# A two-branch attention kernel: the query combine of one branch redone, score banks freed in pairs, and a new instruction order

## Chip, cores, metric

One core of a Trainium2 chip. The metric is the device time of one launch in microseconds. "Before" and "changed" name the two kernels throughout. A launch is called slow when it is over 1.5% above the fastest of its kernel; every profiled launch was fast. Medians and ranges below are over all launches. Same, faster and slower are at 2%.

## The reference, cut to what matters

Both branches read the same x (2048 tokens, 640 columns, 32 heads of 20); a sigmoid gate g mixes them. Branch A is linear attention with a feature map made of two softmaxes:

```python
pq = einsum('bhsd,hdf->bhsf', q, w_phi)                 # pk the same from k
phi_q = concatenate([softmax(pq), softmax(-pq)], -1)    # 40 features per head
kv  = einsum('bhsf,bhsd->bhfd', phi_k, v);  z = phi_k.sum(s)
num = einsum('bhqf,bhfd->bhqd', phi_q, kv)
den = einsum('bhqf,bhf->bhq', phi_q, z) + 1e-6
a = (num / den) @ wo
# branch B: causal softmax attention in 4 segments of 512 tokens, plus a memory term, @ wo
return g * a + (1 - g) * b
```

Write E+ for exp(pq), E- for exp(-pq), Z+ and Z- for their sums over a head's 20 features. Since num and den are both linear in phi_q, a common factor cancels: multiply by Z+, and only E- needs the ratio r = Z+/Z-. Both kernels use that. They differ in where the ratio is applied.

In all views PE is TensorE's matmuls and PEld its weight loads, DVE is VectorE, ACT ScalarE and POOL GpSimd. SBUF is the on-chip memory; PSUM is the memory that TensorE writes to, here eight banks, handed out singly, as four pairs, or four banks at once. Evacuating means copying a result out of PSUM.

## The kernel before

The program is a list of operations with priorities and estimated durations. A scheduler in the kernel's own Python lays them out greedily on each engine when the program is built, and gives them SBUF slots and PSUM banks. A "step" is one group of four heads in one segment of branch B: 32 steps, each with three bursts of score matmuls, five exponentials, four masks and an attention product. Everything else (projections, branch A) fills in between as "fillers". "Burst N" below, and in the prediction, is the first score burst of step N.

```python
def d_act(n): return 0.22 + n * 0.000833            # the scheduler's estimates, us
def d_mm(*ns): return sum(max(n / 2400.0 + 0.004, 0.034) for n in ns)
...
MAXPAIRS = 2                                        # bank pairs that fillers may hold
def filler_ok(self, fillers, t):
    ...
    return len(pairs) <= self.MAXPAIRS              # one-bank tiles
    return len(pairs) < self.MAXPAIRS               # two-bank tiles
...
def burst(js):                                      # in b_step: scores of four heads
    pt = self.pst("QK", 5 if js[0][0] == 2 else 4)  # ONE tile of four banks
    ...
def expair(pt, off, j):
    for p in range(2):                              # two exponentials, two banks each
        self.op("act", d_act(1024), ..., W=[(pt, 2*p), (pt, 2*p+1), (ex, (j, p))])
...
# in a_q(S): query work of branch A, per tile of 128 tokens and half hf of the heads
pt = self.pst("U", 2)                               # bank 0: E+ part, bank 1: E- part
# 22 columns a head: 20 of num, den, and the plain sum Z
recip   sm0 = 1 / U-[:, :, 21]                      # VectorE, 16 elements
mult    sm1 = U+[:, :, 21] * sm0                    # r
mult    W   = U-[:, :, 0:21] * r                    # 336 elements from PSUM
add     W   = W + U+[:, :, 0:21]                    # 336 elements from PSUM
recip   sm2 = 1 / W[:, :, 20]
stt     oA  = W[:, :, 0:20] * g * sm2               # 320 elements
```

The last six lines are VectorE instructions written as formulas; the whole kernel has them as code.

The softmax here doesn't subtract the row's maximum and nothing guards it: scores larger than these inputs give would overflow.

Of the kernel before, what the change touches and what calls it, by code (L numbers as in the profile page):

```python
# [13 lines left out]
D = 640  # L14
# [16 lines left out]
def d_act(n):  # L31
    return 0.22 + n * 0.000833
# [6 lines left out]
def d_pool(n, ins=1):  # L39
    return 0.22 + n * 0.00087 * ins  # L40


def d_mm(*ns):
    return sum(max(n / 2400.0 + 0.004, 0.034) for n in ns)
# [7 lines left out]
class Tile:  # L52
    def __init__(self, name, shape, dtype, pool):
        self.name, self.shape, self.dtype, self.pool = name, shape, dtype, pool
        self.ops = []
        self.h = {}
        self.slot = None
        self.prev = ()
        self.t = None
        self.left = 0  # L60
# [39 lines left out]
class Graph:  # L100
# [33 lines left out]
    def schedule(self):  # L134
# [21 lines left out]
        def dep_time(o, e):  # L156
            m = 0.0
            for d in o.deps:
                t = d.end
                if d.stream == e and e == "pe" and not d.dma:  # L160
                    continue
                if d.dma:
                    t = d.end + 0.1
                elif d.stream != e:
                    t += LAT
                else:
                    t += 0.03
                if t > m:
                    m = t
            return m  # L170

        def tile_avail(t, commit=False):
# [5 lines left out]
            if isinstance(p, PsumPool):  # L178
# [18 lines left out]
                if n == 2:  # L197
                    if not pairs or not self.filler_ok(fillers, t):
                        return None
# [34 lines left out]
        def claim_banks(t, bs):  # L234
# [6 lines left out]
            if t.shape < 4:  # L241
                fillers.add(t)

        def est(o, e):
            st = max(free[e], dep_time(o, e))
            for t in o.claim:
# [4 lines left out]
            for t in o.tiles:  # L251
# [5 lines left out]
                elif t.prev:  # L257
                    for d in t.prev:
                        if d.stream != e:
                            st = max(st, d.end + LAT)  # L260
# [74 lines left out]
    MAXPAIRS = 2  # L335
# [110 lines left out]
class GatedMix(Graph):  # L446
# [40 lines left out]

    def memory(self):
# [19 lines left out]
        self.KVZ1 = fx("KVZ1", [128, 2, NCH, 8, 22], BF16)  # L508
# [14 lines left out]
        self.onec = fx("onec", [128, 1], BF16)  # L523
        self.p_exp = self.pool(2, 10240)
# [11 lines left out]
        self.p_W = self.pool(2, 1344)  # L536
# [4 lines left out]
        self.p_as = self.pool(4, 192)  # L541
# [40 lines left out]
    def dma(self, q, o, i, R=(), W=(), pr=0.0, nbytes=0, transpose=False, noncontig=False, name="dma", after=(), claim=()):  # L582
# [8 lines left out]
        return self.op(q, 0.6 if q != "pool" else 1.0, fn, R, W, pr, name=name, dma=True, lat=2.0 + nbytes / 180e3, after=after, claim=claim)  # L591

    def setup(self):
# [5 lines left out]
        for s in range(SEG):  # L599
            sl = slice(LSEG * s, LSEG * (s + 1))  # L600
            self.dma("sp", xT[:, :, sl], x2d[sl, :], W=[(xT, s)], pr=-30 + 2.5 * s, nbytes=655e3, transpose=True, name=f"x{s}")
            if s == 0:
                self.dma("sp", self.wkT[:, :, :], wqkv[0:D, D:2 * D], W=[(self.wkT, "*")], pr=-29, nbytes=819e3, transpose=True, name="wkT")
        self.dma("sp", self.wqT[:, :, :], wqkv[0:D, 0:D], W=[(self.wqT, "*")], pr=-15, nbytes=819e3, transpose=True, name="wqT")
        self.dma("act", self.stq[:, :, :], wsrc(ins["B_wq"]), W=[(self.stq, "*")], pr=-40, nbytes=819e3, name="stq")
        self.dma("act", self.stk[:, :, :], wsrc(ins["B_wk"]), W=[(self.stk, "*")], pr=-39, nbytes=1638e3, name="stk")
        self.dma("act", self.WvB[:, :, 0:D], wsrc(ins["B_wv"]), W=[(self.WvB, "w")], pr=-38, nbytes=2400e3, name="WvB")
        self.dma("pool", self.WvB[:, :, D:D + 1], ins["gate_w"].rearrange("(c p o) -> p c o", p=128, o=1), W=[(self.WvB, "g")], pr=-40, noncontig=True, name="gw")
        self.dma("pool", self.beta[:, :], ins["B_beta"].partition_broadcast(128), W=[(self.beta, "*")], pr=-39, noncontig=True, name="beta")
        self.dma("pool", self.wphi[:, :, :], ins["A_w_phi"].rearrange("h d f -> (h d) f").rearrange("(c p) f -> p c f", p=128), W=[(self.wphi, "*")], pr=-38, noncontig=True, name="wphi")  # L610
        self.dma("act", self.WvA[:, :, :], wsrc(wqkv[:, 2 * D:3 * D]), W=[(self.WvA, "*")], pr=-30, nbytes=2400e3, name="WvA")
# [30 lines left out]
        op("act", 0.3, lambda e: e.activation(gh2[:, 1, :], self.beta[:, :], ACT.Exp, scale=-1.0), R=[(self.beta, "*")], W=[(gh2, "*")], pr=-20)  # L642
        op("dve", 0.1, lambda e: e.tensor_scalar(gh2[:, 1, :], gh2[:, 1, :], 1.0, None, op0=ALU.add), W=[(gh2, "*")], pr=-20)
        op("dve", 0.4, lambda e: e.reciprocal(gh2[:, 1, :], gh2[:, 1, :]), W=[(gh2, "*")], pr=-20)
        op("dve", 0.1, lambda e: e.tensor_scalar(gh2[:, 0, :], gh2[:, 1, :], -1.0, 1.0, op0=ALU.mult, op1=ALU.add), W=[(gh2, "*")], pr=-20)
# [5 lines left out]
        op("dve", 0.2, lambda e: e.tensor_copy(self.KVZ1[:, 0, :, :, 21], Mk[:, :, :]), R=[(Mk, "*")], W=[(self.KVZ1, "o0")], pr=2)  # L651
        op("dve", 0.2, lambda e: e.tensor_copy(self.KVZ1[:, 1, :, :, 21], Mk[:, :, :]), R=[(Mk, "*")], W=[(self.KVZ1, "o1")], pr=2)
# [7 lines left out]
    def fuse(self, wT, Wd, ic, pr):  # L660
# [12 lines left out]
        self.op("pe", 6 * 0.075, mm, R=[(wT, "*"), (BD, "*")], W=[(pt, 0), (pt, 1)], pr=pr, name="fuse")  # L673
# [3 lines left out]
    def evac(self, n, o, i, W, pr, name="ev", R=()):  # L677
        op = self.op(("act", "dve"), {"act": d_act(n), "dve": d_dve(n, 1, True)}, None, R=R, W=W, pr=pr, name=name)
# [67 lines left out]
    def b_mem(self, n):  # L746
# [7 lines left out]
        for tl in range(4):  # L754
# [9 lines left out]
            self.op("pe", 8 * 0.065, tr, R=rk + [(self.ident, "*")], W=[(pt, 0)], claim=[pk, tm], pr=pr, name="ktr")  # L764
            self.op("act", d_act(1024), lambda e, pt=pt, pk=pk: e.activation(pk[:, :], self.pb(pt, 0, 0, 1024), ACT.Exp),
                    W=[(pt, 0), (pk, "*")], pr=pr, name="pkexp")
            self.op("dve", d_dve(1024, 1, True), lambda e, pt=pt, tm=tm: e.tensor_scalar(tm[:, :], self.pb(pt, 0, 0, 1024), 1.0, 1.0, op0=ALU.add, op1=ALU.max),
# [14 lines left out]
        self.op("pe", 32 * 0.05, mm, R=[(p, "*") for p in pks] + [(vt, tl) for tl in range(4)] + [(vt, "one")], W=[(mp, 0), (mp, 1)], pr=pr, name="Mmm")  # L782
# [32 lines left out]
    def b_step(self, n, g):  # L815
# [7 lines left out]
        def burst(js):  # L823
            pt = self.pst("QK", 5 if js[0][0] == 2 else 4)

            def mm(e):
                for (j, c0) in js:
                    N = LSEG - 128 * j
                    for i in range(4):
                        r = e.matmul(self.pf(pt, i, c0, N), lhsT=qk[32 * i:32 * i + DH, g, 1, 128 * j:128 * (j + 1)],  # L830
# [3 lines left out]
            self.op("pe", 0.18 + sum((LSEG - 128 * j) / 2400.0 + 0.05 for j, _ in js), mm, R=rqk, W=[(pt, i) for i in range(4)], claim=[ex], pr=s, name=f"QK{n},{g}")  # L834
            return pt

        def expair(pt, off, j):
            for p in range(2):
                self.op("act", d_act(1024), lambda e, p=p: e.activation(  # L839
                    ex[:, 2 * p:2 * p + 2, off:off + 512], self.pbanks(pt, 2 * p, 2, 512), ACT.Exp, scale=scale),  # L840
                    W=[(pt, 2 * p), (pt, 2 * p + 1), (ex, (j, p))], pr=s + 0.01 * p, name="exp")
# [11 lines left out]
        p2 = burst([(2, 0)])  # L853
# [10 lines left out]
        for b in range(2):  # L864
# [25 lines left out]
            self.op("pe", cnt * 0.034 + (0.1 if am else 0), pv, R=R, W=[(ad, b)], pr=s + 0.9, claim=[self.oB], name=f"PV{n},{g}")  # L890
# [47 lines left out]
    def b_out(self, n):  # L938
        oB = self.oB
        for qi in range(4):  # L940
# [4 lines left out]
            def tr(e, qi=qi, pt=pt):  # L945
                for c in range(NCH):
                    r = e.transpose(self.pb(pt, 0, 128 * c, 128), oB[:, qi, 128 * c:128 * (c + 1)], self.ident[:, :])
                return r
            self.op("pe", 5 * 0.065, tr, R=[(oB, (g, qi // 2)) for g in range(NG)] + [(self.ident, "*")], W=[(pt, 0)], claim=[oT], pr=pr, name="oTBtr")
            self.evac(640, lambda oT=oT: oT[:, :, :], lambda pt=pt: self.pb(pt, 0, 0, 640).rearrange("p (c s) -> p c s", s=128),  # L950
                      W=[(pt, 0), (oT, "*")], pr=pr, name="oTB_ev")
            self.oTB[4 * n + qi] = oT

    def a_k(self, t):
        pr = 0.8 + 0.75 * t
# [33 lines left out]
    def a_kv(self, S):  # L989
        pr = 0.8 + 0.75 * (4 * S + 4)  # L990
        ts = [4 * S + i for i in range(4)]
        for s in range(2):
# [9 lines left out]
            self.op("pe", 20 * 0.075, mm, R=[(self.Et[t], s) for t in ts] + [(self.vt[t], "*") for t in ts], W=[(pt, 0), (pt, 1)], pr=pr, name="kv")  # L1002
# [11 lines left out]
        def half(hf, first):  # L1014
            lo = 64 * hf
            for k, t in enumerate(ts):
# [4 lines left out]
                else:  # L1021
                    self.op("dve", d_dve(1280, 2), lambda e, src=src: e.tensor_tensor(acc[lo:lo + 64, :], acc[lo:lo + 64, :], src(), ALU.add),  # L1022
# [6 lines left out]
    def a_fin(self):  # L1029
        pr = 12.9  # L1030
# [20 lines left out]
    def load_wo(self):  # L1051
        wsrc = lambda w: w.rearrange("(c p) n -> p c n", p=128)
        deps = list(self.WkA.ops) + list(self.WvA.ops)
        self.dma("sp", self.Wo[:, 0:NCH, :], wsrc(self.ins["A_wo"]), W=[(self.Wo, 0)], pr=13, nbytes=819e3, name="WoA", after=deps)
        self.dma("sp", self.Wo[:, NCH:2 * NCH, :], wsrc(self.ins["B_wo"]), W=[(self.Wo, 1)], pr=13, nbytes=819e3, name="WoB", after=deps)
# [6 lines left out]
    def a_q(self, S):  # L1062
        pr = 13.2 + 4.5 * S
        xT = self.xT
        ETs = []
        for c in range(NCH):
# [8 lines left out]
            self.op("pe", d_mm(*[512] * 5), mm, R=[(self.WqA, ic) for ic in range(NCH)] + [(xT, S)], W=[(pt, 0)], claim=[ET], pr=pr + 0.3 * c, name="pqA")  # L1075
            for s in range(2):
                self.op("act", d_act(512), lambda e, s=s, ET=ET, pt=pt: e.activation(ET[:, s, :], self.pf(pt, 0, 0, LSEG), ACT.Exp, scale=1.0 - 2.0 * s),  # L1077
                        W=[(pt, 0), (ET, s)], pr=pr + 0.3 * c, name="qexp")
            ETs.append(ET)
        K1 = self.KVZ1  # L1080
        kall = [(K1, ("z", 0)), (K1, ("z", 1)), (K1, ("kv", 0)), (K1, ("kv", 1)), (K1, "o0"), (K1, "o1")]
        for tl in range(4):
            t = 4 * S + tl
            oA = self.sbt("oA", [128, D], BF16, self.p_oA)
            pru = pr + 1.5 + 0.75 * tl
# [134 lines left out]
```

## Time and profile before

| | before |
|---|---|
| launches | 441.27 to 447.99 us, median 446.89 (3) |
| span of the profiled run (launch of 443.43 us) | 441.5 us |
| mean granted TensorE clock | 0.872 |

The lines that carry the reading stand in the prediction. "Busy" is the share of the span in which an engine had an instruction; the chain is the path of work and waits that ended last, followed backwards; a waits line says which engine waited for what, for how long in total, how often, and the longest. Two more tables will be needed, so they are given here. The first is a table of windows of the kernel before, cut at score bursts 1, 19 and the last one (columns: window, length, busy us and count of PE, PEld, DVE, ACT, POOL, granted clock, DMA share, GB/s):

```profile
38.57:275.12 236.55, 189.25 (x2086) 110.42 (x2115) 173.63 (x296) 162.41 (x212) 83.08 (x85) 0.91 0.14 29
275.12:413.89 138.77, 108.62 (x1332) 65.62 (x1345) 95.39 (x248) 92.23 (x115) 34.81 (x52) 0.81 0.04 13
413.89:441.50 27.61, 19.15 (x208) 12.07 (x209) 9.84 (x23) 9.12 (x11) 2.55 (x4) 0.74 0.07 24
```

In the first stage no engine is above 80%; in the second the clock averages 0.81, so part of TensorE's busy time is slow time.

### The profile page before, as it was taken

The numbers are of one execution on the slowest core, as the hardware profiler recorded it, in microseconds if no ns is written. First come the engines' busy times: TensorE is split into PE (matmuls) and PEld (weight loads), VectorE is DVE, ScalarE is ACT, GpSimd is POOL, SyncE is SP. The second block draws the span as 40 slices with busy tenths as digits, with TensorE's granted clock in tenths as the row PEclk, the third lists the DMA queues.
The fourth block names the chain that finished last, engine by engine and source line by source line (L and its number), as shares of the span: only waits on it lengthen the run. The fifth ranks groups of instructions, "written<-read, shape, count | busy, mean of one in ns | idle before, by whom it ended". The sixth has DMA issues, their size and how long they took to land.

```text
span 441.5 us, 8777 instructions
## 1 busy us (share of the span) xinstructions
PE 335.6 (76%) x3716; PEld 197.5 (45%) x3762; DVE 287.6 (65%) x584; ACT 274.3 (62%) x356; POOL 131.0 (30%) x163
## 2 busy tenths in 40 slices
PE   0198889596697788686878797877898688867667
PEld 0144454443373446344336454544545364534343
DVE  1321597957866868799428878778733598648940
ACT  1147858565646874577594577678487846477622
POOL 8100643423414441655120122132222212142310
PEclk9999999888698898699689999799898859865569
DMA  8993100410000000044100014000000000000001
GB/s 223 275 189 44 48 3 3 78 27 0 1 16 1 1 0 16 2 150 75 31 0 3 0 25 97 16 16 16 16 30 4 1 1 31 16 15 2 1 1 59
DMA packets 25799, 16.97 MB, mean 38 GB/s; under 512 B 17665, under 2 KB 23585, under 8 KB 25761
## 3 DMA queue, kind: packets, MB, share of 16 engines
q1 hardware_dynamic: 23040, 13.11, 13.4%
q10 hardware_dynamic: 2624, 3.28, 2.3%
q8 instruction: 29, 0.48, 0.4%
q0 software_dynamic: 96, 0.04, 0.2%
q14 instruction: 10, 0.07, 0.1%
HBM read 6.92 MB, written 4.59 MB: 26 GB/s over the span
## 4 chain that ended last, share of the span: by engine, by line
PE 44%; DVE 38%; ACT 9%; DMA 3%; issue 3%; POOL 1%; SPq 1%; POOLq 0%; ACTq 0%
PE ps L698 7%; PE ps L1139 7%; PE ps L968 5%; DVE acc L1022 5%; PE ps L1072 5%; ACT expT L839 4%; PE ps L884 4%; DVE cb L930 4%; DVE z L981 3%; DMA wkT<-in_A_wqkv_dram 3%; PE ps L719 3%; PE ps L1140 2%; DVE W L1110 2%; DVE W L1107 2%; PE ps L830 2%
## 5 line engine op out<-in xcount | busy, mean ns | idle before, releaser
L844 POOL TENSOR_SCALAR_AFFINE_SELECT expT<-expT 128x512 bf16<-128x512 bf16 x128 | 88.9, 697 | 266.5 <-ACT expT L839 216.1
L839 ACT ACTIVATE expT<-ps 128x1024 bf16<-128x1024 f32 x128 | 124.3, 1023 | 31.7 <-PE ps L830 31.5
L884 PE MATMUL ps<-v1B,expT 128*128 128x21 bf16 x1280 | 42.3, 175 | 10.5 <-POOL expT L844 8.0
L698 PE MATMUL ps<-xT,WB 128*128 128x512 bf16 x188 | 49.1, 402 | 1.3 <-issue 0.5
L884 PEld LDWEIGHTS ps<-v1B,expT 128*128 128x128 bf16 x1280 | 39.5, 98 | 18.5 <-POOL expT L844 11.1
L830 PE MATMUL ps<-qk 20*128 20x128 bf16 (+3 forms) x512 | 38.8, 338 | 8.8 <-ACT expT L839 5.8
L858 ACT ACTIVATE expT<-ps 128x1024 bf16<-128x1024 f32 x32 | 32.7, 1022 | 10.9 <-PE ps L830 10.9
L983 POOL TENSOR_TENSOR E<-E,z 128x1280 bf16<-128x1280 bf16 x12 | 30.0, 2496 | 21.9 <-DVE z L982 19.0
L1022 DVE TENSOR_TENSOR acc<-acc,E 64x1280 bf16<-64x1280 bf16 x31 | 31.6, 1018 | 0.8
L968 PE MATMUL ps<-WvA,xT 128*128 128x512 bf16 x74 | 26.7, 443 | 4.7 <-DVE cb L930 3.3
L1072 PE MATMUL ps<-xT,WqA 128*128 128x512 bf16 x95 | 27.9, 443 | 2.8 <-ACT expT L858 1.1
L698 PEld LDWEIGHTS ps<-xT,WB 128*128 128x128 bf16 x200 | 19.0, 102 | 23.1 <-issue 6.0
L1077 ACT ACTIVATE ET<-ps 128x512 bf16<-128x512 f32 x40 | 23.2, 600 | 8.5 <-PE ps L1072 8.1
L1097 PE MATMUL ps<-KVZ,ET 128*128 128x154 bf16 x192 | 20.7, 262 | 9.7 <-DVE W L1110 4.5
L682 ACT ACTIVATE out<-ps 128x640 bf16<-128x640 f32 x13 | 9.2, 704 | 29.5 <-PE ps L1140 29.5
L975 ACT ACTIVATE E<-ps 128x640 bf16<-128x640 f32 x32 | 22.6, 707 | 7.3 <-PE ps L969 7.0
L981 DVE TENSOR_REDUCE z<-E 128x64 f32<-128x1280 bf16 x16 | 23.6, 1478 | 4.9 <-ACT E L975 4.7
L682 ACT ACTIVATE qk<-ps 128x512 bf16<-128x512 f32 x29 | 17.3, 599 | 14.4 <-PE ps L698 13.5
L968 PE MATMUL ps<-WkA,xT 128*128 128x512 bf16 x73 | 23.5, 403 | 3.2 <-DVE vA L683 1.2
L1139 PE MATMUL ps<-Wo,oTA 128*128 128x512 bf16 x71 | 24.1, 422 | 1.1 <-DVE W L1110 1.1
L719 PE MATMUL ps<-WvB,xT 128*128 128x512 bf16 x75 | 23.5, 394 | 1.9 <-ACT v1B L682 1.1
L830 PEld LDWEIGHTS ps<-qk 20*128 20x128 bf16 x512 | 10.5, 94 | 31.7 <-ACT expT L839 13.2
(119 smaller groups left out, 655.5 us busy)
## 6 DMA issues: line engine op xcount, KB each, us to landing
out_dram<-out SPq DMA_DIRECT2D x16, 160.0 KB, 3.4
scr<-qk SPq DMA_DIRECT2D x16, 120.0 KB
qk<-scr SPq DMA_DIRECT2D x16, 120.0 KB
stq<-in_B_wq_dram ACTq DMA_DIRECT2D x1, 800.0 KB, 4.8
stk<-in_B_wk_dram ACTq DMA_DIRECT2D x1, 800.0 KB, 9.6
WvB<-in_B_wv_dram ACTq DMA_DIRECT2D x1, 800.0 KB, 11.6
WvA<-in_A_wqkv_dram ACTq DMA_DIRECT2D x1, 800.0 KB, 13.8
Wo<-in_A_wo_dram SPq DMA_DIRECT2D x1, 800.0 KB, 4.8
```

The source lines that it names most:

```text
L698: r = e.matmul(self.pf(pt, 0, 0, LSEG), lhsT=self.WB[:, w, kc, 128 * c:128 * (c + 1)], rhs=xT[:, kc, LSEG * n:LSEG * (n + 1)], start=(kc = ...
L719: e.matmul(self.pf(pt, 0, 0, 512), lhsT=l, rhs=self.WvB[:, kc, 0:512], start=(kc == 0), stop=(kc == 4))
L830: r = e.matmul(self.pf(pt, i, c0, N), lhsT=qk[32 * i:32 * i + DH, g, 1, 128 * j:128 * (j + 1)], rhs=qk[32 * i:32 * i + DH, g, 0, 128 * j:L ...
L839: self.op("act", d_act(1024), lambda e, p=p: e.activation(ex[:, 2 * p:2 * p + 2, off:off + 512], self.pbanks(pt, 2 * p, 2, 512), ACT.Exp, ...
L844: self.op("pool", d_pool(n_el), lambda e: e.affine_select(view(), view(), pattern=pat, compare_op=ALU.is_ge, fill=0.0, base=0, channel_mul ...
L858: return e.activation(ex[:, :, 1024:1280].rearrange("p (k b) c -> p k b c", k=2), src, ACT.Exp, scale=scale)
L884: r = e.matmul(self.pf(ad, b, 84 * q2 + 21 * i, 21), lhsT=ex[:, i, c0:c0 + 128], rhs=vt[:, j, h, :], start=(j == 0), stop=(j == qi), skip_ ...
L968: e.matmul(self.pf(pt, 0, 0, 512), lhsT=l, rhs=W[:, kc, 0:512], start=(kc == 0), stop=(kc == 4))
L981: self.op("dve", d_dve(1280), lambda e: e.tensor_reduce(z[:, :], Ev(), axis=AX.X, op=ALU.add), R=[(E, 0), (E, 1)], W=[(z, "*")], claim=[rz ...
L1022: self.op("dve", d_dve(1280, 2), lambda e, src=src: e.tensor_tensor(acc[lo:lo + 64, :], acc[lo:lo + 64, :], src(), ALU.add), R=[(self.Et[t ...
L1072: r = e.matmul(self.pf(pt, 0, 0, LSEG), lhsT=self.WqA[:, kc, 128 * c:128 * (c + 1)], rhs=xT[:, kc, LSEG * S:LSEG * (S + 1)], start=(kc == ...
L1139: e.matmul(self.pf(pt, 0, 0, 512), lhsT=l, rhs=self.Wo[:, c, 0:512], start=(c == 0), stop=(c == 9))
```

## The change

The diff holds five things; its core:

```diff
 # 1 combine: Z sums for a whole segment, ratio spread over channels, applied to E- once
+zmm: 40 matmuls, lhsT=ET[c][:, s, tile], rhs=Mk (0/1 head mask), -> Z+ and Z-
+op("dve", ..., reciprocal(rr[:, :, 0, :], Z(1)))        # 128 elements
+op("dve", ..., rr1 = rr0 * Z(0));  rh = bf16(rr1), bf16(rr1 - rh0)   # ratio as two bf16
+rtr: 4 transposes of rh;  evacuate to rT [64, 512]
+for c in range(5): pt = matmul(lhsT=Bsel[:, c, :], rhs=rT)           # spread, 512 columns
+    op("dve", ..., ET[c][:, 1, :] = ET[c][:, 1, :] * pt)
-for hf in range(2): ... reciprocal, mult, mult, add, reciprocal, scalar_tensor_tensor
+for each tile: 12 matmuls accumulate E+ and E- parts into the same columns
+    reciprocal(sm, U[.., DH]);  sm *= g;  oA = U[.., 0:DH] * sm       # 640 elements
 # 2 banks
-    pt = self.pst("QK", 5 if js[0][0] == 2 else 4)
+    pa, pb = self.pst("QKa", 2), self.pst("QKb", 2)     # third burst keeps one tile
+    pa.qk = pb.qk = True                                # not counted as fillers
-MAXPAIRS = 2
+MAXPAIRS = 3
+    ... attention product: after=[self.lastqk]          # behind the step's last burst
 # 3 start: order of loads, first work on TensorE
-x part 0, wkT, x parts 1..3, wqT
+x parts 0, 1, wkT, x parts 2, 3, wqT;  each load's latency set by hand
 # 4 the scheduler's estimates
-return 0.22 + n * 0.000833
+return 0.18 + n * 0.000826        # likewise d_pool, d_mm, transposes, attention products,
+elif d.stream == "pe": t += 0.2   # and 0.2 us after a matmul instead of 0.09
 # 5 priorities of branch A
-key work 0.8 + 0.75 * t, query work 13.2 + 4.5 * S
+key work 1.0 + 1.0 * t,  query work 17.4 + 4.5 * S
```

## The prediction

> **What bounds the kernel now.** I read the page first (busy time, then the slices, then the chain), because the first question is whether one engine is full.
>
> ```profile
> span 441.5 us, 8777 instructions
> PE 335.6 (76%) x3716; PEld 197.5 (45%) x3762; DVE 287.6 (65%) x584; ACT 274.3 (62%) x356; POOL 131.0 (30%) x163
> ...
> PEclk9999999888698898699689999799898859865569
> ...
> PE 44%; DVE 38%; ACT 9%; DMA 3%; issue 3%; POOL 1%; SPq 1%; POOLq 0%; ACTq 0%
> ```
>
> None is full. The chain that ended last changes hands between TensorE (44%) and VectorE (38%): in-order engines that wait for each other, with two places that stand out. The first is the start. The waits say:
>
> ```profile
> PE ps L669 <- DMA wkT<-in_A_wqkv_dram: 20.0, 1, 20.0
> ACT expT L839 <- PE ps L830: 31.5, 30, 4.1
> ACT expT L858 <- PE ps L830: 10.9, 12, 4.1
> PEld ps L830 <- ACT expT L839: 13.2, 23, 1.6
> ```
>
> TensorE's first 20 us are one wait for a transposed weight. The other three rows belong to the softmax ring of branch B: exponentials wait 42.4 us for score matmuls, and score matmuls 13.2 us for exponentials that hold the score banks. The second place is the end, in a table of windows (columns: window, its length, busy us and count of PE, PEld, DVE, ACT, POOL, then the granted clock, DMA share, GB/s):
>
> ```profile
> 392.00:400.00 8.00, 5.14 (x75) 2.91 (x73) 7.45 (x20) 5.08 (x6) 2.68 (x4) 0.50 0.01 2
> 400.00:408.00 8.00, 5.81 (x78) 3.60 (x79) 7.00 (x20) 5.95 (x8) 2.93 (x4) 0.50 0.00 1
> 408.00:416.00 8.00, 5.88 (x85) 3.67 (x82) 7.11 (x20) 4.97 (x6) 2.55 (x4) 0.50 0.01 2
> 416.00:424.00 8.00, 3.91 (x77) 2.43 (x73) 6.34 (x15) 3.45 (x4) 2.55 (x4) 0.50 0.01 2
> ```
>
> Here VectorE is 79 to 93% busy, TensorE has gaps and its clock has fallen to half. What fills VectorE there is the combine that the change redoes, as the groups by shape show (busy us, mean ns):
>
> ```profile
> L1113 DVE SCALAR_TENSOR_TENSOR oA<-W,g,as 128x320 bf16<-128x320 f32 x32 | 18.4, 574 | 1.1
> L1107 DVE TENSOR_TENSOR W<-ps,as 128x336 f32<-128x336 f32 x32 | 16.2, 507 | 1.1
> L1110 DVE TENSOR_TENSOR W<-W,ps 128x336 f32<-128x336 f32 x32 | 16.1, 503 | 1.0
> L1112 DVE RECIPROCAL as<-W 128x16 f32<-128x16 f32 x32 | 8.1, 253 | 1.1
> L1105 DVE RECIPROCAL as<-ps 128x16 f32<-128x16 f32 x32 | 8.0, 250 | 1.9 <-PE ps L1097 1.7
> L1106 DVE TENSOR_TENSOR as<-ps,as 128x16 f32<-128x16 f32 x32 | 5.6, 174 | 1.1
> ```
>
> **What the Trainium skill says.** (1) "VectorE: DVE Perf Modes", section on the perf-mode tiers: a two-tensor operation with a PSUM operand stays at one element per cycle. The trace agrees: 128x336 takes 507 ns and 128x640 takes 824 ns, 1.04 ns per element plus 0.16 us. So the new multiply by a PSUM ratio pays full price. (2) "TensorE: Matmul & The Clock Gate", part on what's actually happening: the array runs at half clock after an idle window and at full clock after a busy one. The windows above agree (0.50 with gaps, back to 1.00 in the final projection after 432 us). (3) Same page, "Wait — 56ns, not 53.3ns?": starts of tiny matmuls are never closer than about 25 ns. Here groups of 128x21 matmuls took 42.3 us for 1280, 33 ns each; this prices the 160 new tiny matmuls. (4) "Perfetto Trace Analysis", Identifying the Most-Contended Engine: matmul busy time misjudges distance from the roof. I therefore count TensorE below by columns at full clock, not by its 76%.
>
> **The change, part by part.**
> 1. Combine, VectorE. Removed: the six groups above, 72.4 us. Added per tile of 128 tokens (16): a reciprocal of 32 elements, 0.35 us (as the 128x32 reciprocal of branch B), a scaling by the gate, about 0.19, and one 640-element multiply from PSUM, 0.82: 1.36 x 16 = 21.8 us. Added per segment (4): reciprocal of 128 elements, about 0.95 (16, 32, 64 elements take 250, 352, 552 ns), three small operations, about 0.7, five 512-element multiplies from PSUM, 0.16 + 512 x 1.04 ns = 0.69 each: 5.1 x 4 = 20.4 us. Net of the combine: -30 us. The order of the built program also moves evacuations between VectorE and ScalarE (oTB copies on VectorE 7 to 13, v and qk two more each, output three to one): about +6 on VectorE, -7 on ScalarE. VectorE ends near 264, ScalarE near 267.
> 2. Combine, TensorE. The 192 matmuls of the combine stay, each a little narrower. Added: 160 sums per head, 160 x 33 ns = 5.3 us; 20 spreading matmuls of 512 columns, 20 x 0.216 = 4.3; 16 small transposes, about 1. Columns divided by 2.4 GHz, all matmuls: about 277 us before, 286 after.
> 3. Score banks. Two of the three score bursts of a step now hold two bank pairs as separate tiles, so a pair goes to the next user after its own exponential, not after both; and other users may fill three pairs. The waits it can touch are the 42.4 and 13.2 us above; I expect perhaps a third of the former, some 12 us, since the burst still needs two free pairs at once.
> 4. Start. The first TensorE work is now the segment-0 projection. It needs x (issue ends at 5.7 us; the weight transfer was usable 3.1 us after its issue, so about 9 us) and the copied query weight (lands at 5.6, two copies of 1.2 and 0.8: about 8). TensorE starts near 9 to 10 instead of 20. Before the first score burst stand ten more value matmuls and fewer fusing ones, +2 us, so that burst moves from 38.6 to about 29.5.
> 5. Order. Query work of branch A now starts at the 19th score burst, not the 14th. This is the part that worries me.
>
> **The sum, by stages.** I cut the instruction order at score bursts, and price each instruction by the measured rows. Stage one, burst 1 to 19 (38.6 to 275.1, 236.5 us): VectorE work 170 then 169, ScalarE 175 then 178, TensorE at full clock 161 then 139. Twenty-two microseconds of TensorE work leave it. ScalarE at 74% now; with freer banks and less TensorE work ahead of each burst I take 80%: 178/0.80 = 222. Stage two, burst 19 to the end (166.4 us): VectorE 96 then 76, ScalarE 100 then 93, TensorE 99 then 131. TensorE becomes its bound. Its best mixed stretch now (burst 16 to 19, 236.6 to 275.1) did 28.6 us of full-clock work in 38.5, 74%; with VectorE relieved and the clock up I take 79%: 131/0.79 = 166. So stage two stays as long although it holds more. Sum: 29.5 + 222 + 166 = 417.5 as span; launches read about 2 us more than the span, and I shade 3 down for the half-clock stretch: **416 us**, against 446.89 recorded (443.4 in the profiled run), 6 to 7% faster.
>
> **The rivals.**
> - TensorE becomes the bound at poor density. For it: +32 us of TensorE work in stage two, and after the last attention product the new order still has all four tiles' combines, transposes and final projections of the last segment (oTB transposes, combine, 80 final matmuls), where before only the transposes and 80 finals stood there (about 19 us). If stage two runs at today's 60%, it takes 218 us and the kernel slows to about 465; at 70%, 187, and about 438, the edge of "same". Against 60%: its worst part was the half-clock stretch, caused by VectorE's chain that shrinks.
> - The new ratio chain (sums, four small VectorE operations, transpose, evacuation, spreading, five multiplies, about 9 us from end to end) stalls each segment's combine: up to 4 x 5 us if the order puts little beside it. The order puts score bursts and projections between for segments 1 to 3, so I give it 5 us; then about 421.
> - Everything fits better: the clock stays up, the score ring closes, ScalarE reaches 85% in stage one (209) and TensorE 83% in stage two (158): about 398.
> - The VectorE saving is hidden and only the start counts: -9, about 437.
>
> **Range and chances.** The favourable rival sets the low end, 399; slow stage two or hidden saving the high end, 434. Launches of one kernel spread by 1.5% here, which is within that. Two per cent faster means below 438: only the 70% case or worse fails it. Faster 0.88, same 0.09, slower 0.03.
>
> **What would show it.** TensorE's first matmul at 9 to 10 us; burst 1 near 29.5, burst 19 near 251. VectorE busy 258 to 270. Exponentials' wait for score matmuls near 28. Clock above 0.87 on the mean, and no 30 us stretch at 0.50. The prediction is wrong if burst 19 comes after 262 (bank pairs did nothing), if the first burst isn't before 33, or if stage two is longer than 180 us with TensorE gaps ended by the ratio chain.

## The result, and the profile after

Ratios here are the mean time of one kernel's fast runs over that of the other's of the same rounds, so not quite the ratio of the medians.

| | before | changed |
|---|---|---|
| launches, median | 445.39 us (4) | 403.24 us (398.73 to 403.72, 4) |
| ratio, 95% interval | | 0.906 [0.895, 0.917] |
| span, clock of the profiled run | 441.5, 0.872 | 401.8, 0.924 |

The changed kernel's page:

```profile
span 401.8 us, 9152 instructions
PE 337.3 (84%) x3958; PEld 196.1 (49%) x3958; DVE 267.4 (67%) x488; ACT 266.4 (66%) x346; POOL 135.5 (34%) x166
PEclk9999988998899789998999989989988997898589
PE 53%; DVE 27%; ACT 10%; DMA 6%; issue 2%; POOL 1%
```

TensorE is busy for nearly the same time (335.6 and 337.3 us; before's trace lacks 46 of 3762 matmul records), VectorE for 20 us less. The 40 us came out of TensorE's idle time: 441.5 - 335.6 = 105.9 before, 401.8 - 337.3 = 64.5 after. On the chain VectorE fell from 38 to 27%.

The same three stages of the changed kernel, again at burst 1, 19 and the last:

```profile
34.47:219.87 185.40, 161.33 (x1916) 93.16 (x1915) 158.00 (x250) 140.70 (x177) 80.83 (x82) 0.94 0.14 30
219.87:368.46 148.59, 131.09 (x1670) 76.97 (x1670) 86.53 (x189) 104.76 (x138) 37.64 (x55) 0.93 0.08 21
368.46:401.80 33.34, 26.10 (x281) 17.17 (x281) 16.17 (x34) 10.73 (x14) 4.44 (x7) 0.75 0.06 21
```

Stage one is 51 us shorter: it holds less work (TensorE 28, ScalarE 22, VectorE 16 us less) and is denser (VectorE 73 to 85%, TensorE 80 to 87%). The rest holds more (TensorE 29, ScalarE 14 us, VectorE 3 less) and is 15.5 us longer, 5.7 of them in the tail.

The waits of the changed kernel that answer to those shown of before:

```profile
PE ps L727 <- DMA xT<-in_A_x_dram: 15.7, 1, 15.7
ACT expT L875 <- PE ps L865: 31.9, 27, 3.6
ACT expT L894 <- PE ps L865: 4.3, 7, 1.0
PEld ps L865 <- ACT expT L894: 6.0, 9, 1.2
```

TensorE's first wait is 4.3 us shorter, not 10; exponentials wait 36.2 us for scores, not 42.4. The new VectorE work by shape:

```profile
L1179 DVE TENSOR_TENSOR oA<-ps,as 128x640 bf16<-128x640 f32 x16 | 13.2, 824 | 0.5
L1153 DVE TENSOR_TENSOR ET<-ET,ps 128x512 bf16<-128x512 bf16 x20 | 12.6, 682 | 4.3 <-PE ps L1151 4.2
L1176 DVE RECIPROCAL as<-ps 128x32 f32<-128x32 f32 x16 | 5.7, 353 | 9.5 <-PE ps L1170 9.4
```

And the end of the changed kernel, in windows:

```profile
368.00:376.00 8.00, 5.68 (x74) 2.76 (x75) 5.10 (x12) 6.37 (x8) 4.59 (x7) 0.50 0.00 0
376.00:384.00 8.00, 5.87 (x81) 5.20 (x79) 4.84 (x11) 1.41 (x2) 0.00 (x0) 0.50 0.01 2
384.00:392.00 8.00, 7.68 (x82) 5.39 (x81) 6.13 (x14) 1.30 (x2) 0.00 (x0) 0.93 0.06 23
```

Before had over 30 us at half clock near its end; now it is 16. VectorE is no longer nearly full there: 61 to 64% at half clock.

### The profile page after: what moved, and what is told of

Same layout as the page of the kernel before. It is cut to its first block, busy times and chain, and to the rows that moved or that the text cites. A ratio compares the mean times of both kernels' runs of the same rounds, so it can differ in the third digit from the quotient of the medians.

```text
span 401.8 us, 9152 instructions
## 1 busy us (share of the span) xinstructions
PE 337.3 (84%) x3958; PEld 196.1 (49%) x3958; DVE 267.4 (67%) x488; ACT 266.4 (66%) x346; POOL 135.5 (34%) x166
## 4 chain that ended last, share of the span: by engine, by line
PE 53%; DVE 27%; ACT 10%; DMA 6%; issue 2%; POOL 1%
PE ps L1205 10%; PE ps L727 8%; PE ps L1109 5%; PE ps L1004 5%; PE ps L920 5%; DVE acc L1058 5%; ACT expT L875 5%; DMA xT<-in_A_x_dram 4%; PE ps L865 3%; ACT expT L894 3%; PE ps L748 3%; DVE z L1017 3%; DVE cb L966 2%; PE ps L1206 2%; DMA acc<-acc 2%; PE ps L1170 2%
## 5 line engine op out<-in xcount | busy, mean ns | idle before, releaser
L880 POOL TENSOR_SCALAR_AFFINE_SELECT expT<-expT 128x512 bf16<-128x512 bf16 x128 | 90.5, 710 | 223.9 <-ACT expT L875 176.8
L875 ACT ACTIVATE expT<-ps 128x1024 bf16<-128x1024 f32 x128 | 123.5, 1024 | 32.2 <-PE ps L865 31.9
L727 PE MATMUL ps<-xT,WB 128*128 128x512 bf16 x200 | 52.7, 407 | 17.9 <-DMA xT<-in_A_x_dram 15.7
L865 PE MATMUL ps<-qk 20*128 20x384 bf16 (+3 forms) x512 | 36.2, 316 | 13.2 <-ACT expT L894 4.3
L894 ACT ACTIVATE expT<-ps 128x1024 bf16<-128x1024 f32 x32 | 32.8, 1024 | 4.9 <-PE ps L865 4.3
L1205 PE MATMUL ps<-Wo,oTA 128*128 128x512 bf16 x80 | 27.5, 428 | 2.3 <-ACT expT L875 1.6
L711 ACT ACTIVATE qk<-ps 128x512 bf16<-128x512 f32 x27 | 15.9, 600 | 19.3 <-PE ps L727 18.9
L1004 PE MATMUL ps<-WkA,xT 128*128 128x512 bf16 x80 | 25.5, 404 | 2.7 <-DVE cb L966 2.1
L1004 PE MATMUL ps<-WvA,xT 128*128 128x512 bf16 x80 | 24.5, 392 | 3.8 <-DVE cb L966 2.3
L748 PE MATMUL ps<-WvB,xT 128*128 128x512 bf16 x80 | 25.7, 403 | 1.2 <-DVE ET L1153 0.6
L1109 PE MATMUL ps<-xT,WqA 128*128 128x512 bf16 x100 | 25.6, 397 | 0.0
L1205 PE MATMUL ps<-Wo,oTB 128*128 128x512 bf16 x80 | 25.3, 402 | 0.0
## 6 DMA issues: line engine op xcount, KB each, us to landing
WvA<-in_A_wqkv_dram ACTq DMA_DIRECT2D x1, 800.0 KB, 15.5
```

What stands on the lines that cost most here:

```text
L727: r = e.matmul(self.pf(pt, 0, 0, LSEG), lhsT=self.WB[:, w, kc, 128 * c:128 * (c + 1)], rhs=xT[:, kc, LSEG * n:LSEG * (n + 1)], start=(kc = ...
L748: e.matmul(self.pf(pt, 0, 0, 512), lhsT=l, rhs=self.WvB[:, kc, 0:512], start=(kc == 0), stop=(kc == 4))
L865: r = e.matmul(self.pf(pts[i][0], pts[i][1], c0, N), lhsT=qk[32 * i:32 * i + DH, g, 1, 128 * j:128 * (j + 1)], rhs=qk[32 * i:32 * i + DH, ...
L875: self.op("act", d_act(1024), lambda e, p=p, pt=pt: e.activation(ex[:, 2 * p:2 * p + 2, off:off + 512], self.pbanks(pt, 0, 2, 512), ACT.Ex ...
L880: self.op("pool", d_pool(n_el), lambda e: e.affine_select(view(), view(), pattern=pat, compare_op=ALU.is_ge, fill=0.0, base=0, channel_mul ...
L894: return e.activation(ex[:, :, 1024:1280].rearrange("p (k b) c -> p k b c", k=2), src, ACT.Exp, scale=scale)
```

## The experiments

The theory at this point: VectorE relief by the new combine carries most of the 42 us. Rivals: the banks, the start, the later place of branch A, or the scheduler's estimates, which change no instruction but the order of all of them. "Undo" runs are the changed kernel with one part as before; "alone" runs are the kernel before with one part as changed. For undo runs I give the ratio against the changed kernel as the quotient of the two ratios against before, since both were measured against before. Each of the two is known to about 1%, so such a quotient is uncertain by some 1.5% (an estimate from the two intervals). Of the five undo runs only u_start's interval lies clear of the changed kernel's, and only just.

### Undoing one part

**u_comb**: the combine of before, all else as changed.

```diff
-zt = self.pst("Zq", 1) ...                 # ratio per segment
+for hf in range(2): ... reciprocal, mult, mult, add, reciprocal, scalar_tensor_tensor
```

> The changed kernel with branch A's query combine as it was (six VectorE groups per half tile, 72 us of VectorE work, no ratio by TensorE), all else as changed: bank pairs, start, priorities, the scheduler's cost numbers. If the combine carries the change (VectorE relief where VectorE was 79 to 93% busy), the time goes back by 20 us or more, to 423 or above. If bank pairs, priorities and cost numbers carry it, the time stays below 412. VectorE busy should be near 290 in both cases.

410.03 us, 0.921 [0.911, 0.932] of before; 0.9212/0.9059 = 1.017 of the changed kernel. VectorE busy is some 29 us above the changed kernel's, but only 1.7% of time went back, with overlapping intervals:

```profile
PE 334.0 (81%) x3762; PEld 191.9 (47%) x3762; DVE 296.1 (72%) x593; ACT 267.2 (65%) x346; POOL 135.1 (33%) x164
```

The theory fails its own test: 423 or more was due.

**u_banks**: score bursts in one tile of four banks, fillers at most two pairs.

```diff
-            if joint:
+            if True:
-    MAXPAIRS = 3
+    MAXPAIRS = 2
```

> The changed kernel with each score burst in one tile of four banks, freed after both exponentials, and at most two bank pairs for other users, as before; combine, start, priorities, cost numbers as changed. If bank pairs carry the change, 420 or more and the exponentials' wait for score matmuls back from 36 to about 42 us or above. If the combine carries it, below 410.

406.28 us, 0.914 [0.907, 0.922]; 1.009 of the changed kernel, and its interval overlaps the changed kernel's. Exponentials waited 23.0 + 9.8 = 32.8 us for scores, less than in the changed kernel:

```profile
ACT expT L875 <- PE ps L865: 23.0, 22, 2.8
ACT expT L894 <- PE ps L865: 9.8, 15, 2.1
```

So within the new order these two pieces are worth next to nothing, and that wait does not measure them. The order of the attention product was left as changed.

**u_prio**: branch A's old priorities.

```diff
-    AK = (1.0, 1.0)
-    AQ = (17.4, 4.5)
+    AK = (0.8, 0.75)
+    AQ = (13.2, 4.5)
```

> The changed kernel with branch A's priorities as before (key work 0.8 + 0.75 per tile instead of 1 + 1, query work from 13.2 instead of 17.4). If moving branch A's work later is what emptied the first stage and closed the gaps, 415 or more. If only the amount of work and the banks matter, 398 to 410.

399.70 us, 0.899 [0.890, 0.908]; 0.992 of the changed kernel, intervals overlapping. In the new order, moving branch A's work later is worth nothing. Alone on the kernel before it was not run, and for the banks that made the difference. The run shows one thing more: it stands at half clock for 32 us, 352 to 384, as long as before did, and is no slower for it. One of those windows:

```profile
360.00:368.00 8.00, 4.58 (x72) 2.02 (x72) 4.23 (x10) 7.72 (x10) 4.70 (x8) 0.50 0.01 2
```

VectorE is 53% busy there, ScalarE 96%.

**u_start**: loads and first work as before.

```diff
-        xload(0, -40, 5.0); xload(1, -39, 5.0); wkT; xload(2, ...); xload(3, ...); wqT
+        x part 0; wkT; x parts 1..3; wqT      # with the old latencies and priorities
```

> The changed kernel with the loads and first instructions ordered as before (transposed key weight second, fusing matmuls first on TensorE). The first score burst stood at 34.5 us against 38.6 before: if these 4 us are worth what they look like, 406 to 409; if the end hangs on something else, 402 to 405. TensorE's first matmul at 20 us.

409.66 us, 0.923 [0.917, 0.930]; 1.019 of the changed kernel, just beyond the 406 to 409 expected. Undone, the start costs about 6 to 8 us; alone on the kernel before it was not run. TensorE's first matmul came at 19.8, the first burst at 38.1.

**u_model**: the scheduler's durations of before.

```diff
-    return 0.18 + n * 0.000826
+    return 0.22 + n * 0.000833
...
-                elif d.stream == "pe":
-                    t += 0.2
-cnt * 0.027 + (0.08 if am else 0)
+cnt * 0.034 + (0.1 if am else 0)
```

> The changed kernel, but the program's scheduler orders it with the durations of before (scalar copies, matmuls, attention products 34 ns a matmul instead of 27, no 0.2 us after a matmul). No instruction is added or removed; only the order, the banks and which of two engines evacuates. The three parts undone alone cost 7 (combine), 3 (banks) and 6 us (start) of 42, so the rest must sit elsewhere: if in these numbers, 420 or more. If the parts replace each other, so that each alone looks small, this too is small: 402 to 412.

410.30 us (403.45 to 415.04), 0.925 [0.913, 0.937]; 1.022 of the changed kernel, with a wide spread. Two of the four launches count as slow; the two fast ones, 403.45 and 408.49, over the fast ones of before (mean 443.40) give 0.916, or 1.011 of the changed kernel. So 2.2% is the high reading and 1.1% the one from fast launches alone. The second reading of the expectation holds: each part undone alone is small. The five undone parts add up to 1.7 + 0.9 - 0.8 + 1.9 + 2.2 = 5.9% (4.8% with the lower reading), not the 10% (0.906 inverted) of the whole.

### One part alone on the kernel before

**d_comb**: only the new combine.

```diff
+zt = self.pst("Zq", 1) ...        # the new a_q, with the priorities of before
-for hf in range(2): ... six VectorE operations
```

> The kernel before, with only the new query combine. If VectorE relief is the change, 420 or below (25 us of VectorE work gone where it was the fullest engine). If it needs the better order around it, 430 to 445. VectorE busy near 262 in both cases.

439.73 us, 0.992 [0.982, 1.002]: same, within the second range expected. VectorE busy fell from 287.6 to 259.4 as expected:

```profile
PE 346.0 (79%) x3958; PEld 201.9 (46%) x3958; DVE 259.4 (59%) x481; ACT 273.0 (63%) x354; POOL 131.5 (30%) x165
```

Where the gain went is seen in the windows. First the kernel before, then d_comb, from 280 to 320 us:

```profile
280.00:320.00 40.00, 32.62 (x417) 19.84 (x422) 31.23 (x81) 26.47 (x33) 9.60 (x14) 0.94 0.05 18
```

```profile
280.00:320.00 40.00, 32.14 (x388) 18.74 (x387) 21.96 (x46) 26.37 (x33) 8.38 (x13) 0.83 0.04 14
```

VectorE fell from 78 to 55% busy, ScalarE did the same 33 instructions, and TensorE did no more: 388 matmuls for 417, busy as long at a clock of 0.83 instead of 0.94. Other stretches were denser (240 to 280 us: 496 matmuls for 406), but over the run the gain is within noise. VectorE's total load was not what set the pace of the old order; its idle time grew instead. The half-clock stretch near the end did not go with it:

```profile
400.00:408.00 8.00, 4.18 (x81) 2.77 (x79) 4.35 (x11) 6.04 (x7) 2.55 (x4) 0.70 0.00 0
408.00:416.00 8.00, 3.95 (x81) 2.45 (x82) 2.12 (x5) 5.97 (x7) 4.41 (x7) 0.50 0.01 2
```

From 384 to 424 us the clock stays at 0.50 to 0.73 with VectorE 26 to 81% busy, where before it was 79 to 93%.

**d_model**: only the scheduler's durations (the edit of u_model in reverse).

```diff
-    return 0.22 + n * 0.000833
+    return 0.18 + n * 0.000826
...
+                elif d.stream == "pe":
+                    t += 0.2
-cnt * 0.034 + (0.1 if am else 0)
+cnt * 0.027 + (0.08 if am else 0)
```

> The kernel before, with only the scheduler's durations of the changed kernel: the same instructions in another order. If the numbers carry the rest, 415 to 430. If the order is not what was lost, 438 to 448.

429.63 us, 0.969 [0.960, 0.977]: faster, by 3%, with the same arithmetic in another order and small shifts between the two engines that evacuate. The new durations are nearer to the trace (an exponential of 1024 elements: 1.073 us estimated before, 1.026 now, 1.023 in the trace). They are a part of the gain that no instruction count shows.

**d_banks**: pairs, third pair for fillers, attention product behind the last burst.

```diff
-pt = self.pst("QK", 5 if js[0][0] == 2 else 4)
+pa, pb = self.pst("QKa", 2), self.pst("QKb", 2);  pa.qk = pb.qk = True
-    MAXPAIRS = 2
+    MAXPAIRS = 3
+    claim=[self.oB], after=[self.lastqk], name=f"PV{n},{g}"
```

> The kernel before, with only the score tiles by bank pair, three pairs for other users, and attention products held behind their last score burst. If the banks were the hidden limit of the old order, 425 or below; if undoing them alone (3 us) tells the truth, 438 to 446.

419.72 us, 0.943 [0.933, 0.954]: 5.7% faster, by far the largest single part, though undoing it cost 0.9%. The next two runs take it apart. They were run on another chip. The third piece, the order of the attention product, leaves the built program unchanged when it is added alone to the kernel before. That doesn't hold beside the other two: d_banks built without it, for this check and not run, has the same 3762 matmuls in another order from the 1612th on, and VectorE gets 11 instructions more. So no run has the two pieces without the third.

**d_split**: only the pair tiles, fillers still at two pairs.

```diff
-pt = self.pst("QK", 5 if js[0][0] == 2 else 4)
+pa, pb = self.pst("QKa", 2), self.pst("QKb", 2)     # MAXPAIRS stays 2
```

> The kernel before with only the two-pair score tiles; other users still at most two pairs, no order of the attention product (that order alone left the built program unchanged, so it needs no run). Banks as a whole gave 23 us on the kernel before. If the early return of a pair is the mechanism, 420 to 428; if it was the third pair for other users, 438 to 446.

449.87 us, 1.018 [1.003, 1.033]: not faster; if anything slower, and above both ranges expected.

**d_max**: only the third pair for fillers.

```diff
-    MAXPAIRS = 2
+    MAXPAIRS = 3                                    # score tiles stay four banks
```

> The kernel before with only the limit for other users raised from two to three bank pairs, score tiles still of four banks. If the third pair is the mechanism, 420 to 428. If the early return is, 438 to 450, and slower than before is possible, because score bursts then find fewer free pairs.

431.82 us, 0.977 [0.963, 0.990]: about 2.3% less time, between the two ranges expected. So neither piece is the mechanism by itself: apart they give +1.8 and -2.3%, together with the order of the attention product -5.7%. The waits of exponentials for scores, d_split, then d_max, then d_banks:

```profile
ACT expT L853 <- PE ps L843: 38.4, 32, 3.6
ACT expT L872 <- PE ps L843: 17.3, 19, 2.7
```

```profile
ACT expT L839 <- PE ps L830: 33.9, 30, 3.1
ACT expT L858 <- PE ps L830: 19.8, 19, 4.6
```

```profile
ACT expT L853 <- PE ps L843: 29.2, 36, 3.0
ACT expT L872 <- PE ps L843: 7.3, 13, 1.1
```

Sums: 55.7, 53.7 and 36.5 us, against 42.4 before. Each piece alone lengthens the score ring's waits; together they shorten them. What d_max gains with longer waits does not show in them. From 80 to 120 us, before, then d_max, then d_banks:

```profile
80.00:120.00 40.00, 27.38 (x296) 15.65 (x292) 30.56 (x43) 24.05 (x29) 15.53 (x15) 0.80 0.15 25
```

```profile
80.00:120.00 40.00, 32.26 (x380) 20.00 (x381) 36.36 (x51) 26.26 (x32) 18.20 (x16) 0.96 0.17 30
```

```profile
80.00:120.00 40.00, 35.46 (x368) 20.52 (x369) 32.78 (x50) 29.71 (x39) 13.10 (x15) 0.91 0.17 30
```

With a third pair, TensorE and VectorE are fuller here (27 to 32 us, 31 to 36 us of 40), and ScalarE, the ring's engine, rises from 24 to 30 us only in d_banks. But d_model, with the banks as before, fills the same stretch as well:

```profile
80.00:120.00 40.00, 32.54 (x365) 18.34 (x364) 35.23 (x47) 30.55 (x37) 18.55 (x19) 0.91 0.15 27
```

So this stretch doesn't tell a gain by banks from one by another order. A reading, argued and not shown bank by bank: fillers in three pairs leave a four-bank burst short of banks, and pair tiles let each pair go to the next user sooner. Why the pieces are worth more together stays open; the order of the attention product is an untested rival.

### The start, and versions that might beat both

**e_start**: the changed kernel with the two value weights loaded on x's queue behind x's first part. In that queue the transposed key weight now also stands before x's second part, not after it. The order on TensorE, VectorE and GpSimd is unchanged.

```diff
-self.dma("act", self.WvB..., pr=-38, lat=12.0);  self.dma("act", self.WvA..., pr=-37, lat=16.0)
+sp queue: x part 0, WvB, wkT, WvA, x parts 1..3, wqT   # model times kept
```

> The changed kernel with the same order on TensorE, VectorE, GpSimd, and on ScalarE but for two loads: the two value weights are loaded on the queue of x, after x's first part, instead of beside it. In the changed kernel TensorE waited for x until 15.7 us. If x was late because other loads shared the transfer engines, TensorE starts at 8 to 12 us and the time falls by 3 to 7 us, to 396 to 400. If the transposing transfer takes that long by itself, it starts at 15 to 16 and the time stays.

394.49 us (392.37 to 399.63), 0.892 [0.880, 0.904]; 0.985 of the changed kernel, the best version run, with intervals that still overlap. Its wait for x:

```profile
PE ps L727 <- DMA xT<-in_A_x_dram: 13.0, 1, 13.0
```

13.0 us instead of 15.7: between the two expectations. The new order of loads brought x 2.7 us sooner; whether by the value weights held back or by the other transposed load behind x, one run can't tell. Most of the 13 us is left with the transfer itself, with the two weights still loaded beside it, or with the transposed load behind it; that is open. The Trainium skill ("DMA: Bandwidth & Descriptors", Issuing engines are not separate DMA queues) says that transfers from different issuing engines run on the same 16 engines and interleave; the 2.7 us fit that, but do not prove it. The first burst moved from 34.5 to 31.1 us. The profiled span fell by 10.7, more than those 3.4; its clock was 0.952 against 0.924. Launches at like clocks differ by about the 3.4: 396.15 us against the changed kernel's 398.73 at 0.939, and 399.63 (counted as slow) against 403.06 to 403.72 at 0.923 to 0.924. So the rest of the 10.7 goes with a clock of 0.952, which two of four launches had and the changed kernel in none of four; whether the loads brought it about is not settled.

**e_both**: those loads, with u_prio's priorities.

```diff
-    AK = (1.0, 1.0);  AQ = (17.4, 4.5)
+    AK = (0.8, 0.75); AQ = (13.2, 4.5)          # and the loads of e_start
```

> The old priorities of branch A (399.7 us when run) and the loads of the run before this in the list together, as a version that may beat both kernels. If both gains add: 392 to 396. If the gain at the start is eaten by later waits: 398 to 401.

396.04 us, 0.896 [0.885, 0.908]: no gain over e_start. The time stands at the edge of the range for gains that add, but the old priorities bring nothing on top.

## Why the prediction was right or wrong

The measured 403.24 us lies in the range, near its favourable rival (398), and 13 below the 416. The direction was right. The reasons are only partly so, and the number is in part luck: of the three terms of the span the start came out 5.0 us longer than predicted, stage one 36.6 shorter and stage two 15.9 longer. Two of its own signs of being wrong came true: the first burst came at 34.5 us (33 was the limit) and stage two took 181.9 (180), though without the ratio chain: TensorE waited for that chain 3.7 us there (multiplies 2.2, ratio 0.8, its evacuation 0.7).

1. **The count of engine work was right.** For the whole run VectorE 264 was predicted, 267.4 measured; ScalarE 267 and 266.4. The pieces too: 682 ns for the 512-element multiply (0.69), 824 for the 640-element one, 353 for the reciprocal.
2. **What the combine is worth failed.** The prediction took the end's 79 to 93% busy VectorE as a bound and made relief there a reason for stage two's density. Alone it gave 0.8% (same), undone 1.7%. A full engine in one stretch and 30 us of work taken from it do not make a gain when the order still waits for other things. The step "half-clock stretch, caused by VectorE's chain" failed with it: in d_comb the clock stayed at 0.50 to 0.73 for 40 us with VectorE far from full. The rival "VectorE saving is hidden and only the start counts" had this part right and the rest wrong.
3. **The banks were under-sized, and by the wrong measure.** "A third of the former, some 12 us" looked at exponentials' waits. In the changed kernel these fell by 6 us; alone, the banks gave 5.7% (some 25 us). The third pair for fillers, dismissed in half a sentence, gave 2.3% alone while that wait grew to 53.7 us.
4. **The start.** The step "about 9 us" for x took the delay between issue and landing, 3.1 us, from another transfer; for x, whose issue ended at 5.7 and which was waited for until 15.7, it was 10. The DMA engines were about as busy in both cases (the DMA share reads 1.06 or more in every 4 us from 4 to 20), so their load in the trace doesn't explain the difference. Term: first burst at 29.5, measured 34.5.
5. **The stage sums.** Predicted 29.5 + 222 + 166; measured 34.5 + 185.4 + 181.9. The term that was mis-sized most is stage one. It put "ScalarE 175 then 178" there. The windows say 162.4 then 140.7, so work had left on all three engines and the 0.80 was put over a numerator that was too big. How the tally came to 175 and 178 is not shown; in the traces, cutting at the last exponential of step 19 instead of at its first burst adds only 8 and 13 us, where 13 and 37 were too many. The right numerator at the same 0.80 gives 140.7/0.80 = 176; measured were 185.4, ScalarE 76% busy. Stage two held what had left: by the prediction's count 131 us of full-clock TensorE work in 181.9, that is 72% and not 79%. The worry about the tail was just: it is 33.3 us, against 27.6, with the last segment's combine in it and half clock for 16 us.
6. **What no step had**: the scheduler's own durations, 3.1% alone and 1.1 to 2.2% undone. The prediction read the order they produced but never counted them as a cause.
7. **Two slips.** With 218 us for stage two the prediction's own sum gives about 468, not 465; nothing rests on it. And where it says that the windows agree with half clock after an idle window, the trace shows the half clock and gaps, but none over 2.13 us from 392 to 424 (see the last section).

Put together: alone, banks, durations and combine multiply to 0.943 x 0.969 x 0.992 = 0.906, the whole gain, which leaves no room for the start, undone at 1.9%. Undone, all five make 4.8 to 5.9%. So the parts overlap; that each new order has other ways round a gap is a likely reason, not a shown one. What stays open is how much of a single part's figure is the part, and how much the luck of a greedy order that is rewritten whenever anything changes; no run measured that luck by itself.

## What to carry to other kernels

Where several engines are at 60 to 80% and none is full, saved work on one of them can turn into idle time: ask first what the order waits for, and test the part alone and undone. Limits on the same buffers can be worth little or do harm when lifted one at a time (+1.8 and -2.3% of time here) and be worth 5.7% when lifted together with an order that fits. And a list scheduler's durations are part of the kernel: ones nearer to the trace moved this one by 3% with the same arithmetic.

## What the Trainium skill lacked or had wrong

- "TensorE: Matmul & The Clock Gate", Part 1, ties the half clock to an idle window of some 3.4 us or, under "A second HAM failure mode", to frequent short idling between groups of matmuls. In the changed kernel the clock read 0.50 from 368 to 384 us while TensorE was busy 5.68 and 5.87 of each 8 us, and its longest gap there was 2.13 us. That is nearer the second case, but the page does not say what share of activity in a window is too little.
- The same page has run-to-run variation for the cold start alone, under 1% of a typical kernel, and tells the cost of dipping in and out of the gate, but not that this cost may vary between launches of one program. Here clock and time vary: the changed kernel's four read clock 0.923 to 0.924 with 403.06 to 403.72 us, and 0.939 with 398.73, which is 1.2% apart. Whether the clock is the whole cause was not tested.
- "DMA: Bandwidth & Descriptors" has the interleaving of queues, but no figure for how late the first of several loads lands when all are issued at once. Here a transposed 640 KB part (512 x 640 x 2 bytes) was waited for until 15.7 us beside four plain loads of 800 KB, and until 13.0 us with two of them queued behind it (and another transposed load next in its queue).
- "Perfetto Trace Analysis", Identifying the Most-Contended Engine, goes by occupancy, and "Optimization Strategy" there says to look for gaps. It has no word on kernels with several engines at 60 to 80% in an order fixed at build time, where relief of one of them can turn into its idle time: VectorE lost 28 us of work in d_comb (287.6 to 259.4) for 0.8% of time, within noise.
